# Attention and two feed-forward layers on one core: the premix moved to the end of its step, and the first two groups of scores sent through DRAM

## The chip, the cores and the metric

The kernel runs on one core of a Trainium2 chip. The core has a matrix engine (TensorE, PE in the profile, with its weight loads shown apart as PEld), a vector engine (VectorE, DVE), an activation engine (ScalarE, ACT), a general engine (GpSimd, POOL) and a queue engine (SyncE, SP) that here issues every DMA. Each engine works through its own instructions in order and waits on semaphores for the others. The metric is the device time of one execution in microseconds; the kernel before takes 1381.3 us in the median of three runs (1380.95 to 1382.7).

## The reference

The computation is an attention with two mixings over the heads, and then two feed-forward layers. Cut to what matters:

```
def _attn_ref(q, k, v, w_pre, w_post):             # batch 4, heads 12, seq 448, head_dim 64
    scores = scale * np.matmul(q, k.transpose(0, 1, 3, 2))
    scores = np.einsum('bhij,hg->bgij', scores, w_pre)      # premix over the heads
    scores = scores - np.max(scores, axis=-1, keepdims=True)
    attn = np.exp(scores)
    attn = attn / (np.sum(attn, axis=-1, keepdims=True) + 1e-09)
    attn = np.einsum('bhij,hg->bgij', attn, w_post)         # postmix over the heads
    return np.matmul(attn, v)
def _moe_ref(x, w1, w2, w3, w_out):                # 1792 tokens, d_model 768, d_ff 1024
    return ((x @ w1) * (x @ w2) @ w3) @ w_out
def _moe2_ref(x, w_in, w_out):                     # d_ff 2048
    h = x @ w_in
    return np.maximum(0.01 * h, h) @ w_out
```

## The kernel before

The attention stage takes the first third of the time, the feed-forward layers the rest; this change touches the attention alone.

**Units of work.** The 448 query rows of a batch are cut into four chunks (three of 120 rows and one of 88). A chunk is cut into blocks of 10 rows, and two blocks make a group (the last group of the short chunk has one). There are 16 chunks, 180 blocks and 92 groups.

**From scores to groups.** `qk` (L199) computes the scores of one pair of heads for a whole chunk (names `pq`, 6 matmuls; two for each of three high and low parts), ACT or DVE copies them to SBUF (`s`), and each pair of two such steps is stored to DRAM (`sdr`, L241, 840 KB a store, three stores a chunk; 616 KB for the short one). `relayout` (L243) reads a group back so that the heads of one query row lie on neighbouring partitions (`sr`, L249, two DMAs of 210 KB a group, five buffers). The first two groups alone take another way: `direct` (L253) copies their rows within SBUF, from `s` to `sr` (L260, four DMAs of 105 KB a group).

**One group.** `premix` (L262) multiplies `sr` by the mixing matrix `kpre` into a PSUM bank per block (`pm`; three banks, so that the second block of a group takes the bank that the first block of the group before had). `softmax` (L273) takes the row maximum on DVE (`mx`, L276) and the exponential with its sum on ACT (`e`, L279). `weigh` (L284) adds 1e-9 to the sum on POOL (`sm`), inverts it on DVE (`rc`, L288) and scales the second mixing matrix by it on POOL (`kr`, L290). `postmix` (L295) multiplies `e` by `kr` (`po`, L304), and a copy brings the result to SBUF (`ap`, L311). When a chunk is through, `av` (L313) multiplies its rows with the values, one pair of heads at a time (`px`, L324, a single PSUM bank for three pairs); after three pairs DVE copies the bank out (`y`, L333; ACT does it for the last chunk).

**The order of the steps.** It is written out by hand (a manual schedule). Before the loop stand the scores of the first two chunks, with `direct(0)` and `direct(1)`, then `relayout` of groups 2 and 3 and `premix(0)`. Step k of the loop (L422 on) then issues: the evictions of the step before, `softmax(k)`, `postmix(k - 1)` interleaved with `weigh(k)`, `premix(k + 1)`, `relayout(k + 4)`, one `qk` of the chunk two ahead (two in some steps, none in step 0 and in the last two chunks), one `av` of the chunk behind (two in some steps, none in the first step of a chunk), then, on the other engines, the copies `y`, the splits of q and k into high and low parts (L79, L179), and a piece of the weight conversion that fills DVE and ACT (L95 to L106, `hl`), whose result goes to DRAM as `wos`. Call t the step's number in its chunk (0 to 5, or 0 to 4).

**After the attention** `fold` (L502) loads `wos` back (L506), loads and converts the first feed-forward weights (`wr`, L87; `wc`, L95 to L106; `ws`, L76 and L79) and multiplies them (`pw`, L517). The order of this stage is set by a scheduler, which uses its own estimates of time; the attention's order is not.

Of the kernel before, what the change touches and what calls it, by code (L numbers as in the profile page):

```python
# [9 lines left out]
F32 = mybir.dt.float32  # L10
# [13 lines left out]
def attention_moe_kernel(ctx: ExitStack, tc, qt, kt, vt, w_pre, w_post, w1, w2, w3t, w_out, w_in2, w_out2, out):  # L24
# [7 lines left out]
    nc = tc.nc  # L32
    B, _, NPAIR, S = kt.shape
# [6 lines left out]
    P = 128  # L40
# [3 lines left out]
    AHEAD, QAHEAD, START = 4, 2, 7  # L44
    HP = 2
    CH = qt.shape[-1]
# [25 lines left out]
    def bank(tag, shape, name):  # L72
        return ps.tile(shape, F32, tag=tag, name=name, bufs=banks[tag])
# [45 lines left out]
    def attention():  # L119
        with ExitStack() as es:  # L120
# [6 lines left out]
            wk = es.enter_context(tc.tile_pool(name="a_wk", bufs=3))  # L127
# [115 lines left out]
            def relayout(k):  # L243

                sr = srt[k] = wk.tile([P, 2, S], F32, tag="sr", name="sr", bufs=5)
                for s, n in enumerate(groups[k]):
                    b, c, o, nb = blocks[n]
                    src = sdr[b, c][o:o + nb].rearrange("(g i) h j -> (i h) g j", g=2)
                    last = nc.sync.dma_start(out=sr[s * Q:s * Q + nb // 2 * H], in_=src)  # L249
                reads.append(last)  # L250
                ends["sync"] = last

            def direct(k):  # L253

                sr = srt[k] = wk.tile([P, 2, S], F32, tag="sr", name="sr", bufs=5)
                for s, n in enumerate(groups[k]):
                    b, c, o, _ = blocks[n]
                    for g in range(2):
                        q0 = o + g * HQ
                        nc.sync.dma_start(out=sr[s * Q:s * Q + HR, g], in_=st[b, c][q0:q0 + HQ])  # L260

            def premix(k):  # L262

                sr = srt.pop(k)
# [48 lines left out]
            def av(b, c, p):  # L313
                c0, ni, _ = chunks[c]
                ap = apt[b, c]
                g, r = divmod(p, 3)
                if p == 0:
                    ys[b, c] = yp.tile([P, NPAIR, CH], F32, tag="y", name="y")
                if r == 0:
                    pxs[0] = bank("px", [P, 3, CH], "px")  # L320
                y, px = ys[b, c], pxs[0]
                for jc in range(NJ):
                    for e in range(2):
                        nc.tensor.matmul(  # L324
                            px[e * D:(e + 1) * D, r, :ni],
                            vst[b][:, jc, 2 * p + e, :],
                            ap[:, jc, 2 * p + e, :ni],
                            start=(jc == 0),
                            stop=(jc == NJ - 1),
                        )  # L330
                if r == 2:
                    copy = nc.scalar.copy if (b, c) == order[-1] else nc.vector.tensor_copy
                    lows.append(lambda: copy(y[:, 3 * g:3 * g + 3, :ni], px[:, :, :ni]))  # L333
                if p == NPAIR - 1:
                    later.append((scr[b][:, :, c0:c0 + ni], y[:, :, :ni]))
# [65 lines left out]
                lo_k[p]()  # L401
            for p in range(NPAIR):
                qk(0, 0, p)
                if p == NPAIR - 1:
                    direct(0)
                flush()
                if p == 0:
                    for low in [k_split(0, 4, nc.gpsimd), k_split(0, 5)]:
                        low()
            q_split(0, 1)()  # L410
            constants()
            direct(1)
            for p in range(NPAIR):
                qk(0, 1, p)
                flush()
            for k in range(2, AHEAD):
                relayout(k)
            q_split(0, 2)()
            premix(0)
            todo = []  # L420
            for k in range(NG + 1):
# [9 lines left out]
                for i in range(2):  # L431
                    if k > 0 and i < len(groups[k - 1]):
                        postmix(groups[k - 1][i], nc.scalar.copy if i and (k == NG or t % 2) else nc.vector.tensor_copy)
                    if k < NG and i < len(groups[k]):
                        weigh(groups[k][i])
                if k + 1 < NG:
                    premix(k + 1)
                if k < NG:
                    if k + AHEAD < NG:
                        relayout(k + AHEAD)  # L440
                    if ci + QAHEAD < len(order):
                        ps = [t] if nt == NPAIR else [4, 5] if t == 4 else [t]
                        if ci == 0:
                            ps = ([], [0], [1], [2], [3], [4, 5])[t]
                        for p in ps:
                            qk(*order[ci + QAHEAD], p)
                    left = nt - t if t else 1
                    for _ in range(-(-len(todo) // left)):
                        av(*todo.pop(0))
                    if t == 0 and k > 0:  # L450
                        todo += [(*where[k - 1][:2], p) for p in range(NPAIR)]
                    if ci + QAHEAD + 1 < len(order) and t == (4 if ci == 0 or c == NC - 2 else 3):
                        lows.append(q_split(*order[ci + QAHEAD + 1]))
                    if b + 1 < B:
                        if c == NC - 3 and t >= 4:
                            lows.append(k_split(b + 1, t - 4))
                        if c == NC - 2 and t < 4:
                            lows.append(k_split(b + 1, t + 2))
# [254 lines left out]
```

## Time and profile before

| | |
|---|---|
| median of three runs | 1381.3 us (1380.95 to 1382.7) |
| the profiled execution | 1380.92 us |
| its span, first to last instruction | 1379.1 us |
| busy: PE, DVE, ACT, POOL | 97%, 64%, 44%, 12% of the span |
| mean granted clock of TensorE | 0.987 |
| DMA | 224.18 MB, mean 163 GB/s |

A row of a timeline gives the start in us, the length in us, the engine, the line, the operation with its output and input, the number of records, and in brackets the idle time ahead of it with what ended that. The PE runs two records for most of the matmuls of the attention, since their operands are of 32 bits, so `x8` at L269 is one group's premix of four matmuls. Matmuls are pipelined: a piece's length overlaps the next piece's start by some 0.07 to 0.09 us. In a table of stretches PEclk is the granted clock, 1.00 for the upper of the two levels (2.4 GHz) and 0.50 for the lower.

### The profile page before, as it was taken

Reading aid. Unit: us, or ns where it says so; the run is one execution under the profiler, and the core shown is the slowest. Engines: PE = TensorE matmul, PEld = TensorE weight load, DVE = VectorE, ACT = ScalarE, POOL = GpSimd, SP = SyncE. Lnnn points to the kernel's source line nnn. Section 1 sums busy time; section 2 is a strip of 40 time slices with the busy share of each in tenths; the row PEclk is TensorE's granted clock in tenths of the full one; section 3 lists DMA queues with packets and bytes.
Section 4 is the critical chain, followed back from the end, with each engine's and each line's share of the span. In section 5 each row is a group of like instructions: output and inputs, shape, how many; then the busy total and the mean of one; then the engine's idle time right before and its main releaser. Section 6 shows DMA issues by size and latency. Waiting matters only on the chain.

```text
span 1379.1 us, 22852 instructions
## 1 busy us (share of the span) xinstructions
PE 1335.9 (97%) x8880; PEld 1128.7 (82%) x8880; DVE 879.3 (64%) x1519; ACT 601.9 (44%) x1163; POOL 166.2 (12%) x371
## 2 busy tenths in 40 slices
PE   5899999999999989999999999999999999999998
PEld 3466666666666679999898999999898989999998
DVE  4366566566566687576347696967665358596862
ACT  4366566556564354333224452443333225453340
POOL 1233333334333300000000000000000000000000
PEclk8799999999999999999999999999999999999999
DMA  5987897797697796433133432427332233342402
GB/s 170 262 292 207 246 308 234 230 313 236 206 281 250 230 294 208 132 93 91 46 119 109 139 115 92 137 90 226 104 111 66 70 115 111 121 135 93 137 1 80
DMA packets 138859, 224.18 MB, mean 163 GB/s; under 512 B 20032, under 2 KB 120384, under 8 KB 138304
## 3 DMA queue, kind: packets, MB, share of 16 engines
q1 hardware_dynamic: 138752, 222.73, 51.9%
q8 instruction: 70, 1.15, 0.3%
q14 instruction: 37, 0.30, 0.1%
HBM read 162.86 MB, written 58.98 MB: 161 GB/s over the span
## 4 chain that ended last, share of the span: by engine, by line
PE 90%; DMA 3%; DVE 2%; SPq 2%; ACT 1%; issue 1%; POOL 1%; ACTq 0%; POOLq 0%; DVEq 0%
PE pm L579 42%; PE po L648 17%; PE po L304 9%; PE pm L269 6%; PE px L324 5%; PE pq L215 5%; PE pw L517 5%; DMA sr<-sdr 1%; SPq L260 1%; ACT e L279 1%; POOL kr L290 1%; DMA wr<-in_moe_w_dram 1%; DVE mx L276 0%; SPq L241 0%; DMA kl<-in_k_dram 0%
## 5 line engine op out<-in xcount | busy, mean ns | idle before, releaser
L579 PE MATMUL pm<-x,ws 128*128 128x512 f32 (+1 forms) x2304 | 466.8, 363 | 0.0
L579 PEld LDWEIGHTS pm<-x,ws 128*128 128x128 f32 x2304 | 417.7, 188 | 47.7
L648 PE MATMUL po<-ws,g 128*128 128x384 f32 x1344 | 234.2, 334 | 0.0
L648 PEld LDWEIGHTS po<-ws,g 128*128 128x128 f32 x1344 | 233.1, 188 | 0.0
L304 PE MATMUL po<-kr,e 128*112 128x120 f32 (+1 forms) x1440 | 176.1, 275 | 2.5 <-POOL kr L290 2.4
L304 PEld LDWEIGHTS po<-kr,e 128*112 128x112 f32 x1440 | 157.2, 179 | 23.4 <-issue 9.7
L79 DVE TENSOR_TENSOR ws<-wc,ws 128x768 fp32r<-128x768 f32 (+1 forms) x104 | 101.3, 976 | 81.5 <-ACT ws L76 81.2
L279 ACT ACTIVATE e<-pm,mx 128x448 f32<-128x448 f32 x180 | 112.6, 632 | 91.1 <-DVE mx L276 90.7
L95 ACT ACTIVATE wc<-wr 128x768 f32<-128x768 f32 (+2 forms) x120 | 104.6, 874 | 82.9 <-DVE ws L79 61.4
L76 ACT ACTIVATE ws<-wc 128x768 fp32r<-128x768 f32 (+1 forms) x104 | 89.1, 859 | 107.4 <-PE po L648 73.9
L269 PE MATMUL pm<-sr,kpre 60*64 60x448 f32 x720 | 119.4, 572 | 17.0 <-DMA sr<-s 6.9
L290 POOL TENSOR_SCALAR kr<-kpost,rc 128x120 f32<-128x120 f32 x180 | 122.9, 683 | 95.9 <-DVE rc L288 43.9
L223 ACT ACTIVATE s<-pq 120x448 f32<-120x448 f32 (+1 forms) x180 | 88.5, 540 | 101.5 <-PE pq L215 101.3
L579 PE MATMUL pm<-h,ws 128*128 128x512 f32 (+1 forms) x576 | 116.3, 363 | 0.0
L276 DVE TENSOR_REDUCE mx<-pm 128x1 f32<-128x448 f32 x180 | 103.9, 617 | 18.5 <-PE pm L269 18.4
L311 DVE COPY ap<-po 112x480 f32<-112x480 f32 (+1 forms) x136 | 88.4, 650 | 41.0 <-PE po L304 38.2
L579 PEld LDWEIGHTS pm<-h,ws 128*128 128x128 f32 x576 | 104.3, 188 | 11.7
L215 PEld LDWEIGHTS pq<-ks,qs 64*120 64x120 f32 (+1 forms) x576 | 48.4, 184 | 76.5 <-issue 55.0
L106 DVE SCALAR_TENSOR_TENSOR wc<-wr,wc 128x768 uint32<-128x768 uint32 (+2 forms) x120 | 110.0, 917 | 1.3
L103 DVE SCALAR_TENSOR_TENSOR wc<-wr,wc 128x768 uint32<-128x768 uint32 (+2 forms) x120 | 109.9, 917 | 1.2
L324 PEld LDWEIGHTS px<-ap,vs 112*64 112x64 f32 x1536 | 74.0, 136 | 31.9 <-issue 24.5
L215 PE MATMUL pq<-ks,qs 64*120 64x448 f32 (+1 forms) x576 | 89.4, 414 | 10.3 <-ACT ks L76 5.8
(51 smaller groups left out, 992.1 us busy)
## 6 DMA issues: line engine op xcount, KB each, us to landing
sr<-sdr SPq DMA_DIRECT2D x172, 210.0 KB
sdr<-s SPq DMA_DIRECT2D x36, 840.0 KB
wr<-in_moe_w_dram SPq DMA_DIRECT2D x32, 768.0 KB
wr<-in_moe_w_in_dram SPq DMA_DIRECT2D x32, 768.0 KB
wr<-in_moe_w_out_dram SPq DMA_DIRECT2D x32, 768.0 KB
wr<-in_moe_w_dram SPq DMA_DIRECT2D x8, 1024.0 KB
sdr<-s SPq DMA_DIRECT2D x12, 616.0 KB
wr<-in_moe_w_out_dram SPq DMA_DIRECT2D x16, 384.0 KB
```

What stands on the lines that cost most here:

```text
L95: nc.scalar.activation(out=cf, in_=hi.bitcast(F32), func=ACTF.Abs)
L103: lambda: nc.vector.scalar_tensor_tensor(out=c, in0=hi, scalar=0xC0000000, in1=c, op0=ALU.bitwise_and, op1=ALU.bitwise_or),
L106: lambda: nc.vector.scalar_tensor_tensor(out=c, in0=lo, scalar=29, in1=c, op0=ALU.logical_shift_right, op1=ALU.bitwise_or),
L215: nc.tensor.matmul(pq[e][:m], qst[b, c][rows, p, x, :m], kst[b, p][rows, y, :], start=(j == 0), stop=(j == 2))
L269: nc.tensor.matmul(pms[n][g * Q:(g + 1) * Q], kpre[rows], sr[rows, g, :], start=True, stop=True)
L276: nc.vector.tensor_reduce(out=mx, in_=pm, axis=AX.X, op=ALU.max, negate=True)
L279: ends["act"] = nc.scalar.activation(out=e, in_=pm, func=ACTF.Exp, bias=mx, scale=1.0, accum_out=sm)
L290: ends["pool"] = nc.gpsimd.tensor_scalar(out=kr, in0=kpost, scalar1=rc, scalar2=None, op0=ALU.mult)
L304: nc.tensor.matmul(po[:, jc].rearrange("p h (g i) -> p h g i", g=2), e[:, jc * JP:(jc + 1) * JP], kr, start=True, stop=True,)
L324: nc.tensor.matmul(px[e * D:(e + 1) * D, r, :ni], vst[b][:, jc, 2 * p + e, :], ap[:, jc, 2 * p + e, :ni], start=(jc == 0), stop=(jc == NJ ...
L579: nc.tensor.matmul(dst, wt[:, a, kk, :], x[:, kk, c, c0:c0 + w], start=(kk == 0 and j == 0), stop=(kk == kn - 1 and j == 2),)
L648: nc.tensor.matmul(po, g[:, m, a, t * P:(t + 1) * P], wts[m][:, c, 0, cs], start=(m == 0 and j == 0), stop=(m == FQ - 1 and j == 2),)
```

## The change

Three edits. The function `direct` goes, and all groups are read back from DRAM by `relayout`; the reads of groups 0 to 3 are issued ahead of the loop that computes the second chunk's scores and stores them. In the loop `premix(k + 1)` stands behind the step's `qk` and `av` instead of ahead of them. In the last chunk the second half of the `av` takes its PSUM bank from the ring of two that the scores used (`qa`) instead of the single bank `px`. Lines behind `direct` move up by 9 to 12 (L269 becomes L260, L304 becomes L295).

```
-            def direct(k):
-                sr = srt[k] = wk.tile([P, 2, S], F32, tag="sr", name="sr", bufs=5)
-                for s, n in enumerate(groups[k]):
-                    b, c, o, _ = blocks[n]
-                    for g in range(2):
-                        q0 = o + g * HQ
-                        nc.sync.dma_start(out=sr[s * Q:s * Q + HR, g], in_=st[b, c][q0:q0 + HQ])
...
-                    pxs[0] = bank("px", [P, 3, CH], "px")
+                    pxs[0] = bank("qa" if g and (b, c) == order[-1] else "px", [P, 3, CH], "px")
...
             for p in range(NPAIR):
                 qk(0, 0, p)
-                if p == NPAIR - 1:
-                    direct(0)
                 flush()
...
             constants()
-            direct(1)
+            for k in range(AHEAD):
+                relayout(k)
             for p in range(NPAIR):
                 qk(0, 1, p)
                 flush()
-            for k in range(2, AHEAD):
-                relayout(k)
             q_split(0, 2)()
             premix(0)
...
-                if k + 1 < NG:
-                    premix(k + 1)
                 if k < NG:
...
                         av(*todo.pop(0))
                     if t == 0 and k > 0:
                         todo += [(*where[k - 1][:2], p) for p in range(NPAIR)]
+                    if k + 1 < NG:
+                        premix(k + 1)
```

On the queue engine SP, at the start of the program, the order before is this (`kl`, `ql` and `wrep` are inputs; `sdr_0` and `sdr_1` are the first two chunks' scores in DRAM):

```order
L189 DMA ql<-in_q_dram 128x720
L241 DMA sdr_0_57<-s 120x1792 x2
L260 DMA sr<-s 60x1x448 x4
L241 DMA sdr_0_57<-s 120x1792
L260 DMA sr<-s 60x1x448 x4
L241 DMA sdr_1_58<-s 120x1792 x3
L249 DMA sr<-sdr_0_57 60x2x448 x6
L189 DMA ql<-in_q_dram 128x720
```

The same place in the changed kernel:

```order
L189 DMA ql<-in_q_dram 128x720
L241 DMA sdr_0_57<-s 120x1792 x3
L249 DMA sr<-sdr_0_57 60x2x448 x8
L241 DMA sdr_1_58<-s 120x1792 x3
L249 DMA sr<-sdr_0_57 60x2x448 x2
L189 DMA ql<-in_q_dram 128x720
```

The third store of the first chunk is no longer behind four copies, and the reads of four groups stand ahead of the second chunk's stores, where before two groups stood behind them.

On PE, in the steps of the first chunks, the order before is this (`pm` is the premix, `pq` the scores, `po` the postmix, `px` the `av`):

```order
L215 MATMUL pq<-ks,qs 120x448 x72
L269 MATMUL pm<-sr,kpre 64x448 x8
L304 MATMUL po<-kr,e 112x120 x8
L269 MATMUL pm<-sr,kpre 64x448 x4
L215 MATMUL pq<-ks,qs 120x448 x6
L304 MATMUL po<-kr,e 112x120 x8
L269 MATMUL pm<-sr,kpre 64x448 x4
L215 MATMUL pq<-ks,qs 120x448 x6
```

And in the changed kernel:

```order
L215 MATMUL pq<-ks,qs 120x448 x72
L260 MATMUL pm<-sr,kpre 64x448 x8
L295 MATMUL po<-kr,e 112x120 x8
L215 MATMUL pq<-ks,qs 120x448 x6
L260 MATMUL pm<-sr,kpre 64x448 x4
L295 MATMUL po<-kr,e 112x120 x8
L215 MATMUL pq<-ks,qs 120x448 x6
L260 MATMUL pm<-sr,kpre 64x448 x4
```

In every step the premix has moved from behind the postmix to the end, behind the scores and (where there is one) the `av`. The orders of DVE, ACT and POOL in the attention are the same as before.

On DVE, where the feed-forward stage begins, the conversions of the first weights (`wr` the words loaded, `wc` the number, `ws` its high and low part) stood so before:

```order
L97 TENSOR_SCALAR wc<-wc 128x1024
L100 TENSOR_SCALAR wc<-wc 128x1024
L103 SCALAR_TENSOR_TENSOR wc<-wr,wc 128x1024
L106 SCALAR_TENSOR_TENSOR wc<-wr,wc 128x1024
L97 TENSOR_SCALAR wc<-wc 128x1024
L100 TENSOR_SCALAR wc<-wc 128x1024
L103 SCALAR_TENSOR_TENSOR wc<-wr,wc 128x1024
L79 TENSOR_TENSOR ws<-wc,ws 128x1024
L106 SCALAR_TENSOR_TENSOR wc<-wr,wc 128x1024
```

In the changed kernel:

```order
L97 TENSOR_SCALAR wc<-wc 128x1024
L100 TENSOR_SCALAR wc<-wc 128x1024
L103 SCALAR_TENSOR_TENSOR wc<-wr,wc 128x1024
L97 TENSOR_SCALAR wc<-wc 128x1024
L106 SCALAR_TENSOR_TENSOR wc<-wr,wc 128x1024
L100 TENSOR_SCALAR wc<-wc 128x1024
L103 SCALAR_TENSOR_TENSOR wc<-wr,wc 128x1024
L106 SCALAR_TENSOR_TENSOR wc<-wr,wc 128x1024
L79 TENSOR_TENSOR ws<-wc,ws 128x1024 x2
```

The scheduler has put one more operation (L106 of the second weight) ahead of the first `ws`. PE's order is the same from the last `av` on.

## Rows read from the trace of the kernel before

**Rows 1.** The page: busy us, share and instructions of each engine.
```profile
PE 1335.9 (97%) x8880; PEld 1128.7 (82%) x8880; DVE 879.3 (64%) x1519; ACT 601.9 (44%) x1163; POOL 166.2 (12%) x371
```

**Rows 2.** Stretches: length, each engine's busy us, PEclk, DMA share, GB/s.
```profile
16.00:20.00 4.00, 3.72 (x19) 2.86 (x21) 3.23 (x10) 1.31 (x3) 0.00 (x0) 1.00 0.72 259
...
24.00:28.00 4.00, 1.90 (x4) 0.38 (x4) 1.08 (x2) 0.72 (x2) 0.23 (x1) 0.83 0.79 195
28.00:32.00 4.00, 1.75 (x2) 0.28 (x2) 0.74 (x3) 0.72 (x2) 0.81 (x2) 0.50 0.33 86
...
36.00:48.00 12.00, 6.59 (x23) 4.14 (x24) 2.14 (x5) 2.02 (x5) 1.63 (x4) 0.50 0.93 288
```

**Rows 3.** Timeline of PE, the first 75 us.
```profile
47.58 2.65 PE L269 MATMUL pm<-sr,kpre 60*64 60x448 f32 x8 [5.41 <-DMA sr<-sdr]
...
51.56 3.05 PE L304 MATMUL po<-kr,e 128*112 128x120 f32 x16
54.54 0.98 PE L269 MATMUL pm<-sr,kpre 60*64 60x448 f32 x8
55.46 0.87 PE L215 MATMUL pq<-ks,qs 64*120 64x448 f32 x6
56.26 1.90 PE L304 MATMUL po<-kr,e 128*112 128x120 f32 x16
...
70.86 0.98 PE L269 MATMUL pm<-sr,kpre 60*64 60x448 f32 x8
```

**Rows 4.** Timeline of SP's queue, the first 80 us.
```profile
12.22 1.36 SPq L241 DMA_DIRECT2D sdr<-s  x2
16.04 6.75 SPq L260 DMA_DIRECT2D sr<-s  x4
...
37.78 7.54 SPq L249 DMA_DIRECT2D sr<-sdr  x6
```

**Rows 5.** Waits of PE and PEld, 56 to 482 us: total, times, longest.
```profile
PE pm L269 <- ACT e L279: 4.6, 10, 0.7
PE px L324 <- DVE y L333: 2.5, 4, 0.6
...
PE po L304 <- POOL kr L290: 2.4, 7, 0.4
...
PEld pm L269 <- ACT e L279: 20.1, 25, 1.4
```

**Rows 6.** Timeline of DVE around one stretched step.
```profile
239.28 0.53 DVE L333 COPY y<-px 128x360 f32<-128x360 f32 x1 [1.53 <-PE px L324]
...
240.19 1.15 DVE L276 TENSOR_REDUCE mx<-pm 128x1 f32<-128x448 f32 x2
```

**Rows 7.** Timeline of PE around the same step.
```profile
238.19 1.04 PE L324 MATMUL px<-ap,vs 112*64 112x120 f32 x16
...
240.98 1.67 PE L269 MATMUL pm<-sr,kpre 60*64 60x448 f32 x8
```

**Rows 8.** Timeline of POOL around the same step.
```profile
233.40 1.30 POOL L290 TENSOR_SCALAR kr<-kpost,rc 128x120 f32<-128x120 f32 x1 [0.36 <-DVE rc L288]
...
242.30 0.59 POOL L290 TENSOR_SCALAR kr<-kpost,rc 128x120 f32<-128x120 f32 x1 [0.36 <-DVE rc L288]
...
243.56 0.74 POOL L290 TENSOR_SCALAR kr<-kpost,rc 128x120 f32<-128x120 f32 x1 [0.36 <-PE pq L215]
```

**Rows 9.** The chain that ended last, 440 to 510 us: start, us, what.
```profile
472.54 3.73 DMA wos<-hl
...
476.67 6.97 DMA wr<-in_moe_w_dram
...
487.53 1.22 DVE wc L106
...
492.54 17.53 PE pw L517 x86
```

**Rows 10.** Timeline of PE at the end of the attention.
```profile
485.10 2.04 PE L324 MATMUL px<-ap,vs 112*64 112x88 f32 x48 [1.82 <-ACT y L333]
```

## The prediction, made before the changed kernel ran

> **What bounds the kernel now.** I read the page first: PE is busy for 97% of the span, so it is PE's remaining idle time and slow time that can go, and every microsecond of either is on the path [rows 1]. Next the stretches, to find where PE is not busy or not at full clock. From 24 to 48 us PE is busy for about half of the time, and from 28 to 48 us its granted clock is 0.50, the lower level of 1.2 GHz [rows 2]. PE's timeline there shows why: group 2's premix waits 5.41 us for its read, and only from 54.5 us on do the steps follow at full clock [rows 3]. SP's timeline gives what stands ahead of that read: four copies issued from 16.04 us take 6.75 us of issue, four more and three stores follow, and the read itself goes out at 37.78 [rows 4]. While the copies run DMA moves 86 GB/s, against 288 later [rows 2]. Then the waits of the 420 us that follow. Their idle gaps are small, but PEld waits 25 times, 20.1 us in all, for the exponential of a group's first block, and PE another 4.6 us: 24.7 us together [rows 5]. One such step shows the cause: the `av` at 238.19 ends, DVE copies `y` at 239.28 and only then starts the row maximum at 240.19, so the premix at 240.98, whose second block needs the bank that this maximum and its exponential free, takes 1.67 us instead of 0.98 [rows 6, 7, 3]. Last the chain where the attention ends.
>
> **The start.** The first chunk's last scores are in SBUF at 16.04, where SP now starts a copy [rows 4]; in the changed kernel the third store stands there. Three stores are 2.58 MB (840 KB each), from 12.2 us on. At the 259 GB/s of 16 to 20 us [rows 2] they need 10.0 us, at 288 GB/s 9.0. A store of 384 KB took 3.73 us [rows 9], 1.5 us of it at 259 GB/s, so I add 2.2 us once for completion: landed at 23.5. The first read (215,000 bytes, 0.8 us, and the same 2.2) lands at 26.5, the eight reads (1.72 MB, 6.6 us) by 33.
>
> PE at half clock then runs: first block's premix, 0.9 us, to 27.4; 2.70 us from a maximum's start to the first `kr` (240.19 to 242.30 plus 0.59 [rows 6, 8]); postmix 0 from 30.1, 3.05 us as the half-clock one at 51.56 [rows 3]; `qk` 1.5 and premix 1.8 (twice the warm lengths); postmix 1 from 36.5 to 39.5. Before it ended at 54.5. That is 15 us.
>
> Not all of it is kept, because the reads that follow stand in one queue. Behind the start of reading at 23.5 and up to group 7 lie 16 reads (3.44 MB), three stores (2.58), one q load (0.37), the values (1.38) and two weight loads (0.79), 8.55 MB. At 259 GB/s that is 33 us and 2.2 us, so group 7 is there at about 59; PE, 15 us ahead, wants it at 70.86 plus 0.9 (it now stands behind a `qk`) less 15, at 56.5 [rows 3]. I take 2.5 to 3 us off: the start gives **12 us**. The ends: 15 with the reads in time; 8 if a read behind stores takes as long as the one issued at 37.78 and landed at 47.4, 9.7 us [rows 4, 3]. Clock and cover: if PE gets its upper level only after a longer run, 2 us of the 15 go.
>
> **The premix at the end of the step.** Nothing is added on any engine; the four matmuls of a group change places. A full step is 1.82 (postmix) + 0.91 (premix) + 0.8 (`qk`) + 0.97 (`av`) = 4.5 us, start to start [rows 3, 7]. Before, the premix came 1.8 us into the step and its second block 0.45 later, while the exponential it needs came on the mean 1.0 us after that when `y` had held DVE up (24.7 us over 25 times, the longest 1.4 [rows 5]). Now it comes 3.6 us in, 1.8 later, and the `av` ends 0.9 us earlier, so `y` and the maximum behind it start earlier too. Either is about the stretch, both are more than the longest: I cost all 24.7 us as gone, and the 2.4 us of `kr` waits [rows 5], which follow the same late maximums.
>
> What is late next is `kr`. The maximum can now start only when a step begins, since its premix ends there; the first `kr` is ready 2.7 and the second 4.1 us later (243.56 plus 0.74, from 240.19 [rows 6, 8]). The postmix that wants them comes one step later, at 4.5 and 5.4: slack of 1.8 and 1.3 us. In the 16 first steps of a chunk there is no `av`, the step is 3.5 long, and the second `kr` is wanted at 4.4; with `y` and a conversion ahead of the maximum it comes up to 0.5 later: 5 us given back. Steps with two `qk` wait for ACT's eviction as before, perhaps 0.3 us more in five of them: 1.5. The 2.5 us of PE waiting for `y` stay, because there two `av` follow each other in one step [rows 5]. Net **20.5 us** (24.7 + 2.4 - 5 - 1.5). Ends: 27 with nothing given back; 5 if DVE, which in such a step has two reciprocals to wait for and then a split, `y` and a conversion to do, all in order, still starts the next maximum a microsecond late.
>
> The longer `kr` shows where this could bite. One at 233.40 took 1.30 us against 0.59 [rows 8]. The Trainium skill (page "SBUF — State Buffer", section "SBUF: two separate sides") says that VectorE, when an instruction reads two SBUF inputs, and GpSimd lock one port pair for a whole instruction, and that the other is held up for that long. By that rule the second `kr` would come at 4.7 instead of 4.1 wherever a split falls beside it, still ahead of 5.4 in a full step, but 0.3 us later in the 16 short ones, 5 us more.
>
> **The end of the attention.** The other PSUM bank takes away the 1.82 us that the last `av` waits for ACT [rows 10]. I cost it at nothing: PE ends there at 487.1 and waits until 492.54 for the first converted weight, whose load was issued at 476.67 behind a store (472.54) that had to land [rows 9]. If that cover were gone it would give 1.8. The store's own source comes behind a `y` copy, so it moves with the steps and some 0.7 us more. Against that, the order on DVE now has one more operation of 1.22 us [rows 9] ahead of the first `ws`. Net **0.5 us** lost; ends 3 lost (more idle time and a longer stretch at half clock behind it) and 2 gained.
>
> **Sum.** 12 + 20.5 - 0.5 = 32 us. The profiled execution took 1380.9, so 1348.9; the median of the runs stands 0.4 above it, so 1349.3. From 492 us on nothing in PE's order changes and PE is fully busy, so what is gained before is kept.
>
> **The rivals.**
> *The start gives little.* The added trip through DRAM costs what the copies cost: 9.7 us a read under load [rows 4, 3] speaks for it; that nothing else is in the queue when the first stores have landed, against. The start then gives 4 to 5 us: 1357.
> *The waits change their name.* `kr` takes the place of `e`: DVE starts the maximum late after every `y`, and the postmix waits instead of the premix. For it: every one of the 25 waits goes back to DVE's order, which is unchanged. Against it: the postmix keeps its place, and the maximum comes 0.9 us earlier behind a `y`. The steady part gives 5: 1364.
> *It doesn't do what it says.* Reads arrive late in many later steps, because DMA is already near its limit in places, and PE's lead is given back: nothing but a few us, 1377. Against it: among PE's waits from 56 us on, whose longest stand in [rows 5], none is for a read.
> *Slower.* The place is the postmix of every step, the price the distance from the end of the premix to the second `kr`. Ahead of the change a maximum could start before its step; now it can't. If the second `kr` came 6.3 us after the maximum instead of 4.1, each of some 70 full steps would wait 0.9 us, 63 in all, against 32 + 5 taken away: 1407. From about 5.9 us on it decides. The row of 4.1 speaks against it.
>
> **How the numbers follow.** My forecast has a chance of 0.66, a slow start 0.12, the renamed waits 0.13, nothing done 0.04, slower 0.05. The range takes the start from 8 to 15 and the steady part from 9 to 27, not both at an end at once: 1339 to 1364, which includes the first two rivals' times. Within 0.2% (2.8 us, about what a measurement here tells from no change) lies only a part of the fourth case: 0.02. Faster 0.93, slower 0.05.
>
> **What would show it.** Right: postmix 1 ends near 40 us instead of 54.5; the clock is at its upper level by 41; PEld's 25 waits for `e` are nearly gone, and a few waits for `kr` appear in the first steps of chunks; the first `pw` starts near 460. Wrong: the first premix starts after 30 us; waits for reads among groups 4 to 8 of over 5 us; PE's or PEld's waits for `kr` of over 10 us; a first `pw` that has not moved by more than the start gives.

## The result, and the profile after

The changed kernel takes 1346.05 us in the median of four runs (1344.58 to 1346.62), the kernel before 1381.24 in runs on the same chip: a ratio of 0.9742 (95% interval 0.9725 to 0.9758), 35.2 us less. 1349.3 had been predicted, with a range from 1339 to 1364. The profiled execution took 1345.55 us, with a span of 1343.8 us and a mean granted clock of 0.992.

The page's first row, of after (busy us, share and instructions of each engine), answers to [rows 1]. The number of instructions is the same on each of these engines; PE's busy time is 23 us shorter: the rows below show less of it stretched by waits and by the lower clock.

```profile
PE 1312.6 (98%) x8880; PEld 1124.0 (84%) x8880; DVE 880.7 (66%) x1519; ACT 601.0 (45%) x1163; POOL 166.0 (12%) x371
```

**The start.** The stretches of after, with the columns of [rows 2]:

```profile
16.00:20.00 4.00, 4.00 (x20) 3.14 (x22) 3.20 (x10) 1.16 (x3) 0.00 (x0) 1.00 0.93 360
20.00:24.00 4.00, 2.85 (x19) 2.37 (x16) 2.50 (x5) 2.81 (x5) 0.00 (x0) 1.00 0.32 115
24.00:28.00 4.00, 2.27 (x8) 0.64 (x8) 1.38 (x2) 0.00 (x0) 0.00 (x0) 0.66 0.99 231
28.00:32.00 4.00, 4.00 (x16) 1.89 (x15) 2.15 (x6) 2.29 (x7) 1.65 (x5) 0.50 0.99 251
...
36.00:48.00 12.00, 12.00 (x106) 7.99 (x98) 8.27 (x19) 8.64 (x22) 5.12 (x12) 1.00 1.02 273
```

The stretch of 86 GB/s has gone. While the first chunk's stores run DMA moves 360 GB/s, then the queue stands nearly still (115 GB/s on the mean of 4 us) until they have landed, and from 36 to 48 us PE is busy without a gap at its upper clock, where before it was busy for 6.59 of 12 us at the lower. PE's timeline of after:

```profile
25.73 5.10 PE L260 MATMUL pm<-sr,kpre 60*64 60x448 f32 x16 [2.88 <-DMA sr<-sdr]
...
30.76 3.54 PE L295 MATMUL po<-kr,e 128*112 128x120 f32 x16
...
36.52 1.90 PE L295 MATMUL po<-kr,e 128*112 128x120 f32 x16
...
55.88 1.65 PE L260 MATMUL pm<-sr,kpre 60*64 60x448 f32 x8 [0.46 <-DMA sr<-sdr]
...
62.76 1.89 PE L295 MATMUL po<-kr,e 128*112 128x120 f32 x16
```

The postmixes of groups 0 and 1 are the second and third row; the latter ends at 38.4, where it ended at 54.54 before [rows 3]. The row at 55.88 is group 7's premix, which meets its read: 0.46 us of idle time, and 1.65 us of length against 0.98 [rows 3]. PE stands idle at no later premix for a read. The last row is group 7's postmix. SP's queue shows the order that brings this about (a row is a run of issues, the last one group 7's read):

```profile
11.94 4.13 SPq L241 DMA_DIRECT2D sdr<-s  x3
22.59 3.56 SPq L249 DMA_DIRECT2D sr<-sdr  x8
26.27 2.11 SPq L241 DMA_DIRECT2D sdr<-s  x3
...
43.10 1.27 SPq L249 DMA_DIRECT2D sr<-sdr  x2
```

Eight reads go out at 22.59, and the first premix runs 3.1 us later. The same postmix of group 7 and the last operation that writes `hl`, in the chain of before (start, us, what):

```profile
77.92 1.82 PE po L304 x16
...
471.97 0.55 DVE hl L79
```

A chain puts the start of a piece of PE where the piece ahead of it ended, here 0.07 us later than a timeline does, so the start of group 7's postmix moves from 77.85 to 62.76: after is ahead by 15.1 us.

**The steps.** Waits of PE and PEld in after, 56 to 430 us (total, times, longest), against [rows 5]:

```profile
PE po L295 <- POOL kr L281: 2.9, 10, 0.5
...
PE pm L260 <- DMA sr<-sdr: 0.5, 1, 0.5
...
PEld po L295 <- POOL kr L281: 32.0, 48, 1.1
```

The 24.7 us of waits for the exponential are gone. The 32.0 us that weight loads now wait for `kr` look like their successor, but a weight load may wait beside the matmuls ahead of it: PE itself waits 2.9 us for `kr`. What a wait of PEld costs must be read from the matmuls that follow. PE's rows for the premix, grouped by line, from the postmix of group 7 to the last `hl`, of before and of after (after the bar busy us, mean ns of a record and idle time):

```profile
L269 PE MATMUL pm<-sr,kpre 60*64 60x448 f32 (+1 forms) x644 | 100.5, 562 | 4.7 <-ACT e L279 4.6
```

```profile
L260 PE MATMUL pm<-sr,kpre 60*64 60x448 f32 (+1 forms) x640 | 80.3, 561 | 0.0
```

20.2 us of the stretching that the weight loads' waits caused have gone, and 4.7 us of idle time. (The mean of a record shows nothing of it: records overlap, and the stretch is in how far apart they start.) Some 0.9 of the 20.2 is no stretch but one premix that now stands behind the last `hl`, and so outside this stretch. Summed over single premixes from 56 us on, the time from the start of one to the next piece, above the 0.91 us of one that waits for nothing, is 27.4 us before and 3.3 after; for the postmixes, above 1.82, it is 5.6 and 7.1. I call these sums the excess of premix and postmix below. The last operation that writes `hl` starts at 471.97 before and at 434.13 after, 37.8 us earlier; 15.1 of it are from the start, so the steps gave 22.7 (with the 0.9 us of the premix that now stands behind it).

**The end of the attention.** The chain that ended last, of after, 434 to 480 us:

```profile
434.13 0.58 DVE hl L79
434.73 3.66 DMA wos<-hl
...
439.28 9.73 DMA wr<-in_moe_w_dram
449.03 1.13 ACT wc L95
...
453.92 1.24 DVE wc L106
...
456.34 23.74 PE pw L505 x120
```

The chain is the one of before [rows 9] up to the conversions of the first weights, and 36.2 us earlier at its end (492.54 to 456.34). The whole span is 35.3 shorter; 2.5 of the 37.8 us are lost here or behind.

### The profile page after: what moved, and what is told of

It reads as the page before. It is cut to its first block, busy times and chain, and to the rows that moved or that the text cites. A ratio compares the mean times of both kernels' runs of the same rounds, so it can differ in the third digit from the quotient of the medians.

```text
span 1343.8 us, 22895 instructions
## 1 busy us (share of the span) xinstructions
PE 1312.6 (98%) x8880; PEld 1124.0 (84%) x8880; DVE 880.7 (66%) x1519; ACT 601.0 (45%) x1163; POOL 166.0 (12%) x371
## 4 chain that ended last, share of the span: by engine, by line
PE 87%; DMA 6%; DVE 2%; POOL 2%; ACT 1%; issue 1%; SPq 0%; POOLq 0%; ACTq 0%; DVEq 0%
PE pm L567 43%; PE po L636 17%; PE po L295 9%; PE px L315 5%; PE pw L505 5%; PE pm L260 4%; PE pq L215 4%; DMA sr<-sdr 1%; POOL kr L281 1%; DMA sdr<-s 1%; DMA ql<-in_q_dram 1%; DMA xm<-scr 1%; DMA wr<-in_moe_w_dram 1%; ACT e L270 1%; DVE mx L267 0%
## 5 line engine op out<-in xcount | busy, mean ns | idle before, releaser
L295 PEld LDWEIGHTS po<-kr,e 128*112 128x112 f32 x1440 | 156.1, 178 | 71.3 <-POOL kr L281 33.1
L295 PE MATMUL po<-kr,e 128*112 128x120 f32 (+1 forms) x1440 | 175.7, 274 | 3.6 <-POOL kr L281 2.9
L106 DVE SCALAR_TENSOR_TENSOR wc<-wr,wc 128x768 uint32<-128x768 uint32 (+2 forms) x120 | 110.2, 919 | 1.3
L215 PE MATMUL pq<-ks,qs 64*120 64x448 f32 (+1 forms) x576 | 90.1, 419 | 10.1 <-ACT ks L76 5.6
L97 DVE TENSOR_SCALAR wc<-wc 128x768 f32<-128x768 f32 (+2 forms) x120 | 64.9, 541 | 50.1 <-ACT wc L95 49.9
L260 PE MATMUL pm<-sr,kpre 60*64 60x448 f32 x720 | 94.3, 571 | 3.3 <-DMA sr<-sdr 3.3
L315 PEld LDWEIGHTS px<-ap,vs 112*64 112x64 f32 x1536 | 73.9, 136 | 25.7 <-issue 17.3
L315 PE MATMUL px<-ap,vs 112*64 112x120 f32 (+1 forms) x1536 | 90.4, 264 | 3.6 <-DVE y L324 2.9
```

Source lines behind the costliest of these rows:

```text
L106: lambda: nc.vector.scalar_tensor_tensor(out=c, in0=lo, scalar=29, in1=c, op0=ALU.logical_shift_right, op1=ALU.bitwise_or),
L215: nc.tensor.matmul(pq[e][:m], qst[b, c][rows, p, x, :m], kst[b, p][rows, y, :], start=(j == 0), stop=(j == 2))
L260: nc.tensor.matmul(pms[n][g * Q:(g + 1) * Q], kpre[rows], sr[rows, g, :], start=True, stop=True)
L295: nc.tensor.matmul(po[:, jc].rearrange("p h (g i) -> p h g i", g=2), e[:, jc * JP:(jc + 1) * JP], kr, start=True, stop=True,)
L315: nc.tensor.matmul(px[e * D:(e + 1) * D, r, :ni], vst[b][:, jc, 2 * p + e, :], ap[:, jc, 2 * p + e, :ni], start=(jc == 0), stop=(jc == NJ ...
```

## The experiments

Each was timed in five or three rounds beside the kernel before on the same chip (medians of before 1380.8, 1381.95 and 1380.05 in the three sessions); ratios are to that kernel, in brackets the 95% interval. Line numbers are those of the kernel shown, so a line may stand some higher or lower than in after.

**1. The move undone (after, with the premix back in the middle of the step).**

```
+                if k + 1 < NG:
+                    premix(k + 1)
                 if k < NG:
...
-                    if k + 1 < NG:
-                        premix(k + 1)
```

> The changed kernel with the premix put back in the middle of the step; the reads through DRAM ahead of the stores, and the other bank, stay. My theory: the start and the move are two gains that add up, 15 us and 22 us. Then this takes 1367 us (1364 to 1370), postmix 1 still ends at 38 to 39 us, and PEld's 25 or so waits for the exponential are back with 20 us. Rival, that the early start is only worth something with the move (the scores no longer wait behind a premix): 1373 or more, and postmix 1 ends after 42.

1366.04 us, 0.9893 (0.9879 to 0.9908): 14.8 us faster than before, as expected. The waits are back, and with them a premix excess of 28.6 us:

```profile
PEld pm L260 <- ACT e L270: 19.4, 24, 1.4
```

**2. The move alone (before, with the premix at the end of the step).**

```
-                if k + 1 < NG:
-                    premix(k + 1)
...
+                    if k + 1 < NG:
+                        premix(k + 1)
```

> The kernel before with the premix at the end of the step and nothing else changed. My theory: the steady steps give their 22 us alone and the start gives 0 to 2: 1358 us (1355 to 1362), PE's stretched premixes gone, waits for kr under 5 us on PE. Rival, that DMA was the limit and only the earlier start made room for the faster steps: 1365 or more, with waits for reads in the steps from 100 us on.

1357.16 us, 0.9829 (0.9813 to 0.9845): 23.6 us faster, as expected, with a premix excess of 3.3. Either edit works without the other: 14.8 and 23.6 are 38.4, and all three edits gave 35.2. The first value holds the new bank too. The profiles put most of these 3 us (2.4) in the end of the attention and none in its steps: from group 7's postmix to the last `hl` it takes 394.0 us in experiment 1 (394.1 before) and 371.3 in experiment 2 (371.4 in after), but from there to the end of the span 905.5 and 908.8 against 907.1 before and 909.7 in after. In experiment 1 the conversions there stand in another order, which the scheduler sets (see the account of the end, below).

**3. The bank undone (after, with one bank for `px` throughout).**

```
-                    pxs[0] = bank("qa" if g and (b, c) == order[-1] else "px", [P, 3, CH], "px")
+                    pxs[0] = bank("px", [P, 3, CH], "px")
```

> The changed kernel with the last av back in its single bank. My theory: worth nothing, since PE waits for the first converted weight anyway: 1346 us, within 1 us of the changed kernel. Rival: the 1.8 us wait for ACT comes back on the path: 1348.

1342.42 us, 0.9723 (0.9707 to 0.974). I had expected no difference to after; it is lower by 0.19% of the time before, but the intervals meet. It was run again beside after (9 and 10).

**4. The reads of the first four groups behind the second chunk's stores (after otherwise).**

```
-            for k in range(AHEAD):
-                relayout(k)
             for p in range(NPAIR):
                 qk(0, 1, p)
                 flush()
+            for k in range(AHEAD):
+                relayout(k)
```

> The changed kernel with the reads of groups 0 to 3 issued behind the second chunk's stores; all groups still go through DRAM. My theory: the order in the queue is what counts, and 2.58 MB of stores take 9 us: first premix at 34 to 36 us instead of 25.7, and 1354 us (1351 to 1357). Rival, that leaving the copies out is the gain wherever the reads stand: 1346 to 1349.

1348.88 us, 0.9761 (0.9745 to 0.9777): only some 3 us are given up. The rival is right. PE's timeline of this kernel:

```profile
31.71 4.99 PE L260 MATMUL pm<-sr,kpre 60*64 60x448 f32 x16 [11.09 <-DMA sr<-sdr]
...
60.31 0.98 PE L260 MATMUL pm<-sr,kpre 60*64 60x448 f32 x8
```

The first premix comes 6.0 us later than in after, not 8 to 10, and group 7's read is there when it is wanted. Stretches of the same kernel show why: the stores follow each other, DMA moves up to 392 GB/s and never stands still, where after has a pause at 115 GB/s for the landing of the first chunk.

```profile
20.00:24.00 4.00, 0.62 (x7) 0.22 (x3) 2.14 (x3) 1.63 (x3) 0.00 (x0) 0.78 0.94 392
24.00:28.00 4.00, 0.00 (x0) 0.00 (x0) 0.00 (x0) 0.00 (x0) 0.00 (x0) 0.50 0.96 330
```

**5. The copies kept (after, with `direct(0)` and `direct(1)` as before, and the reads of groups 2 and 3 ahead of the second chunk's stores).**

```
                 qk(0, 0, p)
+                if p == NPAIR - 1:
+                    direct(0)
                 flush()
...
-            for k in range(AHEAD):
+            direct(1)
+            for k in range(2, AHEAD):
                 relayout(k)
```

> The changed kernel with groups 0 and 1 copied within SBUF as before; the reads of groups 2 and 3 stand ahead of the second chunk's stores. My theory: eight copies hold SP and the queue until 32.6 us whatever follows; postmix 0 stays at 38 us, postmix 1 ends near 47: 1354 us (1351 to 1357). Rival, that only the reads behind the second stores were the loss: 1346 to 1349.

1356.95 us, 0.9821 (0.9806 to 0.9837), 11 us slower than after. SP's queue and PE's timeline of this kernel:

```profile
16.39 6.77 SPq L260 DMA_DIRECT2D sr<-s  x4
...
24.49 8.35 SPq L260 DMA_DIRECT2D sr<-s  x4
32.95 4.47 SPq L249 DMA_DIRECT2D sr<-sdr  x4
```

```profile
39.27 3.54 PE L304 MATMUL po<-kr,e 128*112 128x120 f32 x16
...
67.18 1.87 PE L269 MATMUL pm<-sr,kpre 60*64 60x448 f32 x8 [2.06 <-DMA sr<-sdr]
68.98 3.28 PE L304 MATMUL po<-kr,e 128*112 128x120 f32 x16
```

The copies hold the queue for 1.7 us (the first four) and 2.1 us (the other four) of issue each on the mean, so the reads of groups 2 and 3 go out at 32.95 and group 0's postmix runs 8.5 us later than in after. Then group 7's premix waits 2.06 us for its read, and the postmix behind it takes 3.28 us: a second stretch at the lower clock (a granted clock of 0.55 from 69.0 to 72.2 us). Taken back one at a time, the copies cost some 11 us and the place ahead of the stores some 3 (experiment 4). Seen from experiment 2, which has both as before, taking out the copies alone gives some 9 us (experiment 4), moving the reads alone some 1, which is within the noise (this one), and both 12 (after; all three with the new bank).

**6. The premix between `qk` and `av` (after otherwise).**

```
                         for p in ps:
                             qk(*order[ci + QAHEAD], p)
+                    if k + 1 < NG:
+                        premix(k + 1)
                     left = nt - t if t else 1
                     for _ in range(-(-len(todo) // left)):
                         av(*todo.pop(0))
...
-                    if k + 1 < NG:
-                        premix(k + 1)
```

> The changed kernel with the premix between the step's scores and its av, 0.8 us later than before and not 1.8, and the av and the copy y behind it not earlier. My theory: a stretch lasted 1.0 us on the mean, so taking 0.8 off each leaves 5 to 8 us of the 25 waits: 1351 us (1349 to 1354). Rival, that the gain came from the av and so y and the maximum starting earlier: the waits stay, 1362 or more.

1363.94 us, 0.9869 (0.985 to 0.9888): 18 us slower than after, so the theory falls. The premix is only one `av` earlier than in after, yet nearly all of the gain is gone. Premix excess 14.5, postmix excess 16.8: 31.3 together, against 33.0 before, so the later premix moved the loss more than it removed it. Waits of PE and of DVE, 56 to 430 us, in this kernel:

```profile
PE po L295 <- POOL kr L281: 10.0, 30, 0.8
...
DVE y L324 <- PE px L315: 45.3, 26, 4.0
```

The last row points to the cause. DVE stands for 45.3 us, 26 times, at a copy `y` that waits for the `av` at the end of its step, with the next group's maximum queued behind it. The same wait before and in after:

```profile
DVE y L333 <- PE px L324: 43.6, 25, 4.0
```

```profile
DVE y L324 <- PE px L315: 15.7, 23, 3.0
```

Before it came 25 times, as often as PEld's wait for the exponential [rows 5]. In this kernel the rival of the renamed waits has come true in part: with the `av` last, the `kr` takes the place of `e`. That the wait of DVE is the cause is tested by 7 and 8.

**7. The copy `y` on ACT instead of DVE (experiment 1 otherwise).**

```
-                    copy = nc.scalar.copy if (b, c) == order[-1] else nc.vector.tensor_copy
+                    copy = nc.scalar.copy
```

> The changed kernel with the premix back in the middle of the step (as in the first experiment) and all copies y on ACT instead of DVE. My theory: the waits came from y, which held DVE's maximum behind the av; without y on DVE they go even with the premix in its old place: 1349 us (1346 to 1354) against 1367. Rival, that they come from elsewhere on DVE, or that ACT's exponential is then held up by y in the same way: 1362 or more.

1355.4 us, 0.9808 (0.9793 to 0.9823), between the theory's 1349 and the rival's 1362. The wait went along with the copy. Waits of ACT:

```profile
ACT y L324 <- PE px L315: 75.8, 27, 4.1
```

The maximum is free of it, but the exponential behind it on ACT isn't: premix excess 17.2, postmix excess 9.6. That half of the gain comes speaks for the wait on DVE, but not for what it is worth alone.

**8. The copy `y` behind the next step's maximums, on DVE (experiment 1 otherwise, so with the premix in its old place).**

```
-                    lows.append(lambda: copy(y[:, 3 * g:3 * g + 3, :ni], px[:, :, :ni]))
+                    (lows if (b, c) == order[-1] else late_y).append(lambda: copy(y[:, 3 * g:3 * g + 3, :ni], px[:, :, :ni]))
...
                         postmix(groups[k - 1][i], nc.scalar.copy if i and (k == NG or t % 2) else nc.vector.tensor_copy)
+                    while late_y:
+                        late_y.pop(0)()
                     if k < NG and i < len(groups[k]):
                         weigh(groups[k][i])
...
+                        if todo[0][2] == 3:
+                            while late_y:
+                                late_y.pop(0)()
                         av(*todo.pop(0))
```

> The premix in the middle of the step as in the first experiment (1366 us), and the copy y on DVE, but behind the next step's maximums and first reciprocal instead of at its own step's end. My theory after the run with the premix between scores and av: what cost time is DVE standing still ahead of y until the av is over (43 us in 25 waits in the kernel before, 45 with the premix in between, 16 in the changed kernel), not where the premix stands. Then DVE's waits for px fall under 8 us and this takes 1346 us (1343 to 1350). Rival, that the premix has to be behind the exponential's bank whatever DVE does: 1358 or more, with over 15 us of stretched premixes left.

1341.84 us, 0.972 (0.9707 to 0.9733). The premix stands where it stood before, and all of the gain is there: 24.2 us less than experiment 1 by the medians, below the expected 1343 to 1350, and less than the changed kernel in the same session (0.9755, 0.9742 to 0.9768, intervals apart). Its median is the lowest of all, though experiments 3 and 12 can't be told from it (0.9723 and 0.9721). Premix excess 3.5, postmix excess 6.0. Waits of DVE and PE, 56 to 430 us:

```profile
DVE y L324 <- PE px L315: 4.6, 3, 1.5
...
PE po L295 <- POOL kr L281: 0.7, 3, 0.3
```

So it is not the place of the premix that cost time, but DVE standing still ahead of a copy until an `av` had ended. The change removes that by ending the `av` before the premix; this kernel by copying later. From group 7's postmix to the last `hl` it takes 367.2 us, after 371.4: 3.2 of the 4.2 us are idle time of PE (2.2 of that the waits for `kr`). But these 4.2 us are not what sets it apart from after, since its start gives most of them back. PE's timeline at group 7's read:

```profile
56.02 2.43 PE L260 MATMUL pm<-sr,kpre 60*64 60x448 f32 x8 [2.00 <-DMA sr<-sdr]
...
59.73 3.54 PE L295 MATMUL po<-kr,e 128*112 128x120 f32 x16
```

With the premix early in its step PE meets that read sooner, waits 2.00 us and runs on at a granted clock of 0.50 from 58 to 63 us, so group 7's postmix starts at 66.75, 4.0 us later than in after, and the last `hl` at 433.93, where after has 434.13 (and 435.39 when run again). The rest of the lead lies at the end: from the last `hl` to the end of the span it takes 907.3 us, as before (907.1), and 909.7 and 909.0 in the two profiles of after. The scheduler, which sets the order there, has kept the one of before in this kernel.

**9 and 10. After again, and the bank undone again, side by side.**

> The changed kernel again, beside the one without the other bank on the same chip. My theory: the bank lets PE finish the av 5 us earlier and then stand idle, and the stretch at half clock behind that idle time is 3.4 us longer, so the bank costs time: 1345 to 1347, 2 us or more above the run without it. Rival: the 3.6 us between the two were the chip: within 1 us of each other.

> The changed kernel with the last av in its single bank, again, for the comparison in the same session. My theory: 1342 to 1344, 2 us or more below the changed kernel; in both, what PE does from the first product of the feed-forward stage on is the same but for its clock. Rival: 1345 to 1347.

1346.1 us (0.9755, 0.9742 to 0.9768) and 1344.03 (0.9734, 0.972 to 0.9747): 2 us, as the theory had it, but the intervals overlap, and the traces put most of it elsewhere. Timeline of PE, of after run again, at group 7's read:

```profile
55.50 2.07 PE L260 MATMUL pm<-sr,kpre 60*64 60x448 f32 x8 [1.39 <-DMA sr<-sdr]
57.50 3.05 PE L295 MATMUL po<-kr,e 128*112 128x120 f32 x16
```

The wait is 1.39 us instead of 0.46, and the postmix behind it takes 3.05 us instead of 1.89, the half-clock length of [rows 3] (granted clock 0.60 from 57.5 to 60.5 us); with one bank it was 0.39 and 1.90. So the last `hl` is at 435.39 in the one and 433.95 in the other: 1.4 us that have nothing to do with the bank. At the end of the attention, after run again and then one bank:

```profile
445.73 3.86 PE L315 MATMUL px<-ap,vs 112*64 112x88 f32 x96 [0.65 <-DVE ap L302]
...
454.60 1.65 PE L505 MATMUL pw<-wo,ws 128*128 128x384 f32 x4 [5.00 <-ACT ws L76]
457.78 22.44 PE L505 MATMUL pw<-wo,ws 128*128 128x384 f32 x115 [1.53 <-ACT ws L76]
```

```profile
444.28 2.04 PE L315 MATMUL px<-ap,vs 112*64 112x88 f32 x48 [0.65 <-DVE ap L302]
450.33 3.79 PE L315 MATMUL px<-ap,vs 112*64 112x88 f32 x48 [4.01 <-ACT y L324]
455.56 24.77 PE L505 MATMUL pw<-wo,ws 128*128 128x384 f32 x133 [1.44 <-ACT ws L76]
```

With two banks PE does the last `av` at once and then waits 5.00 us in one piece; with one, the second half waits for ACT and falls into the time in which PE had nothing to do anyway. From the last `hl` to the end of the span it takes 909.7 and 909.0 us in the two profiles of after, 907.5 and 908.9 in the two with one bank. The bank gains nothing, and whether it costs the 1.2 us between the means stays open: they differ by no more than two profiles of one kernel do.

**11. The copy `y` late as in 8, with the premix at the end and one bank (experiment 3 otherwise).** The edit is that of 8.

> The changed kernel without the other bank (1342.4 us in an earlier run) and with y behind the next step's maximums. My theory: DVE's last 16 us of waits for px go too, and with them some of the 7 us of kr waits in the first steps of chunks: 1339.5 us (1337.5 to 1341.5). Rival: these waits are DVE's spare time by now, nothing changes: 1342 to 1343.

1344.3 us, 0.9742 (0.9729 to 0.9756), beside 1344.03 without the late copy: nothing, so the theory falls. The waits of `y` do go, from 15.7 us to 1.0, but they cost nothing any more: the two edits remove the same loss. What is left on DVE is a maximum that waits for its premix, and that is work in PE's order:

```profile
DVE mx L267 <- PE pm L260: 57.9, 58, 3.5
```

**12. The first feed-forward weights loaded ahead of the last load of `wos` (after otherwise).**

```
+                    if kk == KF - 1:
+                        with ExitStack() as behind:
+                            for e in ends.values():
+                                behind.enter_context(tc.issue_after(e.ins))
+                            fill()
```

> The changed kernel with the loads of the first three feed-forward weights issued ahead of the last read of the stored conversion (wo), no longer behind the landing of that store. My theory: the chain from that store to the first converted weight sets when the feed-forward stage starts, and 3.7 us of it are the store's landing: 1342.5 us (1341 to 1344), first pw 3 to 4 us earlier. Rival: the loads only wait elsewhere (DMA is full, or the last read now comes late for the first product): 1346.

1342.37 us, 0.9721 (0.9707 to 0.9735): some 3 us less than after by the ratios, the expected size, but mostly not for the expected reason. PE's timeline:

```profile
446.72 6.62 PE L315 MATMUL px<-ap,vs 112*64 112x88 f32 x96 [3.82 <-DVE ap L302]
...
454.78 25.51 PE L510 MATMUL pw<-wo,ws 128*128 128x384 f32 x144 [1.44 <-ACT ws L76]
```

The first `pw` was to start 3 to 4 us earlier; it starts 1.6 us later (453.17 in after) and goes on without a break, so the long `pw` starts 1.6 us earlier than in after, and 0.9 of that it already had at the last `hl` (433.22), where no edit was made. But the scheduler put a conversion that waits for the weights ahead of the last `ap` on DVE, so the `av` waits 3.82 us and takes 6.62 us (granted clock 0.56; 3.86 us at 1.00 in after), and the `pw` behind it runs at the upper clock from its start (1.00 from 454.8 to 462 us, against 0.56 from 456.3 to 463 in after): from there to the end of the span it takes 885.2 us instead of 887.5. The lower clock fell into a time in which PE had to wait anyway, and the long stage was spared it.

## Why the prediction was right, and where its sizes and reasons were off

**The start, 12 predicted, 15.1 measured.** The steps came as worked out and a little sooner: stores landed and reads out at 22.6 (23.5), first premix at 25.7 (26.5), postmix 1 through at 38.4 (39.5). That is 16.2 us ahead of before instead of 15. The term that was mis-sized is the 2.5 to 3 us given back to group 7's read. It is 1.1 (0.46 of idle time, 0.67 of stretch). The error is in the rate of 259 GB/s, taken from a stretch in which copies already stood in the queue [rows 2]: freed of them the stores ran at 360, reading began 0.9 us sooner, and the read landed at 55.8 instead of 59, which for the 8.55 MB and 2.2 us of the prediction is 276 GB/s. The small size is in part luck: in the profiles of other kernels PE waited up to 2.06 us for the same read. The clock had risen by 36 us, ahead of the 41 I had allowed. What the prediction did not separate are two edits with one aim: leaving out the copies is worth 9 to 11 us, reading ahead of the stores 1 to 3 (experiments 2, 4 and 5). The rival that the trip through DRAM costs what the copies cost is thereby excluded.

**The steps, 20.5 predicted, 22.7 measured.** The 24.7 us went, as forecast: the premix excess fell by 24.1. The step that fails is the reason: "Now it comes 3.6 us in, 1.8 later, and the `av` ends 0.9 us earlier [...] Either is about the stretch". The two are not alike. In experiment 6 the premix is later than before by a `qk`, and the `av` is last again: the premix excess falls by 12.9 us, the postmix excess grows by 11.2. In experiment 8 the premix is not moved at all, and the copy alone gives 24 us. It is the `av` ahead of the maximum, through the in-order queue of DVE, that counts. I had seen that copy in [rows 6] yet took the later premix for a cure by itself. The 5 us given back to late `kr` were too many: by the prediction's own figures the second `kr` came at 4.6 us where 4.4 was wanted, 0.2 in each of 16 steps, which is 3.2, and the postmix excess grew by 1.5. One of the signs of being wrong did show, PEld's waits for `kr` of over 10 us (they are 32.0): the sign was badly chosen, since these waits hardly delay a matmul. The prediction had taken PEld's 20.1 us for `e` as PE's time without showing more than one such step; that was right there, and would have been wrong for `kr`.

**The end, 0.5 lost predicted, 2.5 measured.** From the start of the first conversion by ACT to the long `pw` it takes 10.3 us against 8.9 before: 1.4, near the 1.22 of the extra DVE operation. The other kernels bear this out, since the scheduler gave them different orders: with six operations on DVE ahead of the first `ws` it takes 6.3 and 6.7 us (experiments 1 and 6), with seven 8.9 (before, and experiment 8), with eight and two banks 10.3 to 10.4 (after, experiments 4 and 5). So this loss goes with an order that no edit asked for. 0.9 lie behind the start of that `pw`. The clock fits: of the stretch from 440 to 470 us of after its mean is 0.83, about 10 us at the lower level, and of 470 to 500 before 0.89, 6.6 us; but no run changed that alone. The bank I costed "at nothing", because PE waits there anyway, and the runs show no gain of it, and at most a small loss.

**The sum** came within 3.3 us, with errors of +3.1, +2.2 and -2.0 us, which partly cancel. The slower rival did not come, as the row of 4.1 given against it said: a maximum can't start before its step now, but `kr` stays in time; PE waits 2.9 us for it, 2.4 before. The renamed waits did not come either, though experiment 6 shows how near they are: one swap of `premix` and `av`.

## What to carry to other kernels

When an engine works in order, look for the instruction on it that waits for another engine's late work, and ask what is queued behind it: here a copy nobody was in a hurry for held up a maximum that everything waited for, and issuing the copy later was worth as much as reordering the matrix engine. A wait of the weight loads is no cost until the matmuls behind it are shown to come late. Where an engine waits anyway, shortening its work ahead of that wait gains nothing. Where a scheduler sets the order of a later stage, look at that order in every variant before giving a difference of some microseconds to the edit.

## What the runs showed of the hardware

- Copies within SBUF (60 rows of 448 words from 5 source partitions, 105 KB) took 1.7 to 2.1 us of issue each on the mean of four and moved 86 GB/s at a DMA share of 0.33 [rows 2, 4]; the way through DRAM brought the same rows sooner, with 231 to 251 GB/s from 24 to 32 us in after, and its first premix 3.1 us after the issue. The semaphore of such a copy is stepped six times in the trace of before, that of a store to DRAM or of a read back 16 times. The Trainium skill (page "DMA: Bandwidth & Descriptors", section "Why a DMA increments its semaphore by 16 and not by 1") says that a transfer runs on the largest number of engines, up to 16, that divides the slowest dimension of both its sides; for 5 source partitions and 60 rows that is 5 by our estimate, and the share of 0.33 (5.3 of 16 engines) agrees.
- In stretches of stores to DRAM, DMA moved 360 GB/s (after, 16 to 20 us) and 392 (experiment 4, 20 to 24 us); in those of the reads that regroup the scores, with the next stores queued behind them, 231 to 251 (after, 24 to 32 us).
- Short waits of PE could have a price beyond their length. Behind group 7's read the next postmix took 3.05 us after a wait of 1.39 (after run again), 3.41 after 1.69 (experiment 6), 3.54 after 2.00 (experiment 8) and 3.28 after 2.06 (experiment 5), with granted clocks of 0.50 to 0.60; but 1.90 after 1.54 in experiment 1 and 1.89 after 0.46 in after, at 1.00. So the length of the wait alone does not tell which it will be. That read met PE at another moment in each profile (waits of 0 to 1.39 us in five profiles of kernels with the same start and order of steps), which alone moves the end by more than a microsecond.
- A matmul on tiles declared float32 left two records in the trace (8 for the four of a premix, L260), one on the split tiles declared float32r left one (6 for the six of a `qk`, L215), though both are of 32 bits.
